# Reordering the loads and the normalising in the first fourteen steps of an attention and key-value kernel

## The chip, the cores and the metric

The kernel runs on one core of one Trainium2 chip. The metric is device time in microseconds (us) of a whole launch; the number that counts is the median of the runs. The engines are named as in the profile: PE (matrix products), DVE (vector), ACT (activations), POOL (general purpose) and SP (which here only issues DMAs).

## The reference

Eight batches of twelve heads of attention with a soft cap, followed by a gated two-layer block on the 8 x 448 rows of 768:

```python
scores = cap * tanh((q @ k.T / sqrt(64)) / cap)           # 8 x 12 x 448 x 448
attn = exp(scores - max); attn = attn / (attn.sum(-1) + 1e-9)
x = (attn @ v) as rows of 12 * 64 = 768
xk = mu_k * x + (1 - mu_k) * x_prev                       # x_prev: the row before
xr = mu_r * x + (1 - mu_r) * x_prev
k = relu(xk @ w_k)                                        # 768 -> 1024
out = sigmoid(xr @ w_r) * (k * k @ w_v)
```

The weights come as 64-bit floats.

## The kernel before

The attention works in 48 pairs of heads, two heads of 448 rows side by side in the partitions. A loop runs over steps i = 0 to 54 (`step`, line 710). What a step does is written out as a string of operation names, and every name emits its instructions at that place, on the queues of the engines that it uses; each engine and each DMA queue works through its own in that order. `STEP_0` serves steps 0 to 5, `STEP_5` step 6, `STEP_6` steps 7 to 13, and `STEP` and `STEP_2` the rest. A name stands for another pair according to the table in `step`: scores (`S`, four groups of keys, three products each of high and low halves), tanh, exp and `red` (sums of exp) take pair i; `V` (the products with v, line 256), `gather`, `recip`, `rec_store` take pair i − 1; `norm` and the mixing take pair i − 2; `qk_high` and `qk_low` split pair i + 2; `load_qk` fetches pair i + 3.

The reciprocal of the row sums takes a way through DRAM: DVE's `red` (line 276) sums over blocks of 32, four DMAs on SP's queue gather them (`gather`, line 283, waiting for the last `red`), DVE adds up, takes reciprocals and transposes (`recip`, line 287), SP stores 3.5 KB to DRAM (`rec_store`) and loads it back spread over the partitions in two DMAs (`rec_load`, line 298; one buffer). `norm` (line 304, DVE) multiplies the products with v by it, `mix_old` (line 307, ACT) and `mix_new` (line 317, DVE) mix neighbouring rows, and POOL splits the result (`x_high`, `x_low`) for the second part.

Beside this a step converts one piece of the weights: load (`weight_load`, SP), absolute value (`weight_abs`, ACT), five roundings on DVE (`fill`, written f in the string), sum and copy on POOL (`weight_sum`, line 469), low half on DVE at the head of the next step (`weight_low`, line 483). The first six pieces have 384 columns, the next ones 768. The first weight piece goes through the roundings in step 0 (`weight_first`).

PE does scores and `V`; from the end of step 6 on it also does `K`, 24 products a step with the first weight matrix, from the mixed rows of six pairs. In steps 7 to 13 its order within a step is scores 0 and 1, `V`, scores 2, K, K, scores 3, K, K. The score buffers are two: scores 0 and 1 of a step need tanh 2 and tanh 3 of the one before. A second stage after the attention multiplies by the other two weight matrices, on PE nearly alone; `out_store` (line 623) writes the result from SP's queue.

Of the kernel before, what the change touches and what calls it, by code (L numbers as in the profile page):

```python
# [10 lines left out]
F32 = mybir.dt.float32  # L11
F32R = mybir.dt.float32r
AF = mybir.ActivationFunctionType
ALU = mybir.AluOpType
# [11 lines left out]
HN = DM // 2  # L26
NU = NT // 256
SLOTS = 7
AHEAD = 2
P = 128  # L30
U32 = mybir.dt.uint32
CAP = 50.0
# [21 lines left out]

STEP = """gather load_v quad_load x_store weight_load weight_low S0 S1 V S2 f f f f f tanh0 exp0 red0
weight_sum tanh1 exp1 red1 norm recip rec_store K qk_high qk_low tanh2 relu mix_old k_store prep mix_new x_high x_low gate_old
K exp2 red2 weight_rest weight_sum relu k_store prep S3 K prep K tanh3 exp3 red3 gate_new relu k_store prep
weight_abs load_qk rec_load quad_load tail_open weight_store"""  # L60
STEP_2 = STEP.replace("K qk_high", "K S3 qk_high").replace("prep S3 K", "prep K")
STEP_0 = """gather load_v x_store weight_load weight_low S0 S1 S2 V f f f f f norm tanh0 exp0 red0 weight_first
weight_sum tanh1 exp1 red1 recip rec_store K qk_high qk_low tanh2 relu exp2 mix_old k_store mix_new x_high x_low gate_old
K red2 weight_rest weight_sum relu k_store S3 K K tanh3 exp3 red3 gate_new relu k_store weight_abs load_qk rec_load weight_store"""
STEP_6 = """gather load_v x_store weight_load weight_low S0 S1 V S2 f f f f f norm tanh0 exp0 red0
weight_sum tanh1 exp1 K relu_early qk_rise tanh2 relu exp2 mix_old k_store mix_new red1 recip rec_store qk_low x_high x_low gate_old
K red2 weight_rest weight_sum relu k_store S3 K K tanh3 exp3 red3 gate_new relu k_store weight_abs load_qk rec_load weight_store"""
STEP_5 = STEP_6.replace("V S2", "S2 V")


def f(ap):
# [3 lines left out]
class Body:  # L75
# [30 lines left out]
    def scale(self, pool):  # L106
        nc = self.nc
        self.scl_t = pool.tile([P, 1], F32, name="scl_t")
        nc.vector.reciprocal(self.scl_t, self.cap_t)
        nc.vector.tensor_scalar(self.scl_t, self.scl_t, D ** -0.5, None, op0=ALU.mult)  # L110

    def consts(self, pool):
        nc = self.nc
        self.mu, self.om = {}, {}
        for n, src in (("k", self.muk), ("r", self.mur)):
            m = pool.tile([P, ND], F32, name="mu_" + n)
            nc.sync.dma_start(m, src)
            o = pool.tile([P, ND], F32, name="om_" + n)
            nc.vector.tensor_scalar(o, m, -1.0, 1.0, op0=ALU.mult, op1=ALU.add)
            self.mu[n], self.om[n] = m, o  # L120
        self.grd = pool.tile([P, 1], F32, name="grd")
        if self.maxima:
            nc.vector.memset(self.grd, 1e-9)
            return
        sq = pool.tile([1, 1], F32, name="sq")
        nc.vector.tensor_mul(sq, self.cap_t[0:1], self.cap_t[0:1])
        nc.vector.tensor_scalar(self.flag, sq, CAP * CAP, None, op0=ALU.is_le)
        nc.vector.tensor_scalar(self.cap_t, self.cap_t, -CAP, CAP, op0=ALU.max, op1=ALU.min)

        nc.scalar.activation(self.grd, self.cap_t, AF.Abs)  # L130
        nc.scalar.activation(self.grd, self.grd, AF.Exp, scale=-1.0)
        nc.vector.tensor_scalar(self.grd, self.grd, 1e-9, None, op0=ALU.mult)


    def init_x(self, pool):
# [23 lines left out]

    def init_attn(self):  # L160
        self.raw, self.QK, self.rawv, self.S, self.P32, self.PV, self.R, self.rs = ({} for _ in range(8))
        self.tails = []

# [128 lines left out]

    def rec_store(self, i):
        self.nc.sync.dma_start(self.rec_d[i].rearrange("h (b k) -> (h b) k", k=32), self.rs.pop(i)[0:NB])

    def rec_load(self, i):
        r = self.up.tile([P, S], F32, name="r", bufs=1)
        for h in range(2):  # L300
            self.nc.sync.dma_start(r[HALF[h]], self.rec_d[i][h:h + 1, :].to_broadcast([64, S]))
        self.R[i] = r
# [320 lines left out]
    def out_store(self, u, key, o, g):  # L623
        self.nc.vector.tensor_mul(o, g, self.vl.pop((u, key)))
        t = ((u - NU) * 2 + key // 2) * P
        self.nc.sync.dma_start(self.out[t:t + P, key % 2 * HN:(key % 2 + 1) * HN], o)

    def v_load(self, u, key):
        t = self.vl[u, key] = self.ldp.tile([P, HN], F32, name="vl", bufs=6)
# [80 lines left out]
    def step(self, i, KS):  # L710

        nk = nq = 0
        if self.maxima and i < NPAIR:
            self.row_maxima(i)
        pair = dict(load_qk=i + 3, qk_high=i + 2, qk_low=i + 2, qk_rise=i + 2, load_v=i, S=i, tanh=i, exp=i, red=i)
        pair.update(dict.fromkeys("V gather recip rec_store rec_load".split(), i - 1))
        pair.update(dict.fromkeys("norm mix_old mix_new x_high x_low gate_old gate_new".split(), i - 2))
        pair["x_store"] = i - 3
        for op in (STEP_0 if i < 6 else STEP_5 if i == 6 else STEP_6 if i < REST[0] else STEP_2 if i % NP == 2 else STEP).split():
            j = pair.get(op)  # L720
            op, g = (op[:-1], (int(op[-1]),)) if op[-1].isdigit() else (op, ())
            if op in pair:
                j = pair[op] if j is None else j
                if i == NPAIR + 1 and op in ("x_high", "x_low"):
                    g = ("s",) if op == "x_high" else ("v",)
                if 0 <= j < NPAIR:
                    getattr(self, dict(S="scores", V="values").get(op, op))(j, *g)
            elif op == "K":
                n = ((i - LAG) * 4 + nk + 1) * KS
                if 0 <= n < B * NF * ND * 3:  # L730
                    self.kpart(n, n + KS)
                nk += 1
            elif op == "tail_open":
                self.tail_open(i)
            elif op == "f":
                if i in (QUADS + 3, QUADS + 5):
                    self.quad_sum(i - QUADS - 3)
                elif i <= NPAIR:
                    self.fill()
            elif op == "quad_load":  # L740
                if QUADS <= i < QUADS + 4:
                    self.quad_load(2 * (i - QUADS) + nq)
                    nq += 1
            elif op == "relu_early":
                if i % NP == 2:
                    self.relu()
            elif op == "weight_load":
                if i + 1 in KEYS or i + 1 in REST:
                    self.weight_load()
            elif op == "weight_first":  # L750
                if i == 0:
                    self.weight_abs()
                    self.weight_rest()
            elif op == "weight_abs":
                if i in KEYS or i in REST:
                    self.weight_abs()
            else:
                getattr(self, op)()

    def run(self):  # L760
        tc, nc = self.tc, self.nc
# [6 lines left out]
        with ExitStack() as outer:  # L768
            def pool(name, bufs, stack=outer, **kw):
                return stack.enter_context(tc.tile_pool(name=name, bufs=bufs, **kw))  # L770
# [9 lines left out]
            cpool = pool("cpool", 1)  # L780
# [20 lines left out]
            first = self.qk_first()  # L801
            self.cap_load(cpool)
            self.load_part(0, slice(S + P, S + KC))
            self.weight_load()
            next(first)
            self.scale(cpool)
            next(first)
            self.consts(cpool)
            self.init_sums(self.xkp[0])
            self.load_qk(1)  # L810
            self.qk_high(1)
            self.qk_low(1)
            self.init_guard()
            self.load_qk(2)
            self.weight_load()
            self.wgen = self.weight_round()
# [124 lines left out]
```

## Time and profile before

| what | us |
|---|---|
| median of three runs (922.75 to 924.2) | 922.76 |
| the profiled execution | 921.6 |
| its span, from the first to the last instruction | 919.7 |
| PE busy in it | 891.4 |
| DVE busy | 739.3 |
| ACT busy | 643.5 |
| POOL busy | 384.8 |

The shares of busy time are averages over two parts of different kind: the attention with the first weight matrix, up to 554 us, with all engines at work, and the second stage. The change is in the first 135 us and at the last store, so the profile is read there by stretches, and PE's 97% of the whole says little about it.

### The profile page before, as it was taken

The page shows a single profiled execution, that of the slowest core. Times are in us where ns is not written, and L with a number is a line of the kernel's source. Part 1 is how long each engine was busy: PE and PEld are TensorE (multiplying, and loading weights), DVE is VectorE, ACT ScalarE, POOL GpSimd, SP SyncE. Part 2 cuts the span into 40 slices and gives each one's busy share as a digit, 9 for nine tenths or more (in the row PEclk, how much of TensorE's full clock was granted, in tenths as well). Part 3 has the DMA queues.
Part 4 walks back from the last instruction along what each step waited for, and adds up shares of the span by engine and source line. Part 5 has one row for each costly group of instructions (what it writes and reads, how often), then busy time and mean ns, then how long its engine had stood idle before and what let it go on. Part 6 is the DMA issues. An engine that isn't in the chain of part 4 may idle for free.

```text
span 919.7 us, 15134 instructions
## 1 busy us (share of the span) xinstructions
PE 891.4 (97%) x4986; PEld 716.0 (78%) x4986; DVE 739.3 (80%) x1253; ACT 643.5 (70%) x949; POOL 384.8 (42%) x332
## 2 busy tenths in 40 slices
PE   6879999999999999999999999999999999999996
PEld 3335677666666776666677799999999999999996
DVE  6999977888888888888878866788778767777775
ACT  7978888888887887888877666565565535555553
POOL 4655554776676676666764300000000014443330
PEclk9989999999999999999999999999999999999998
DMA  5565544666566666666656474745454646666663
GB/s 180 153 188 187 187 143 159 223 214 202 197 194 209 213 192 207 207 193 205 196 187 194 128 237 153 234 158 170 154 168 143 189 134 192 217 219 219 218 214 104
DMA packets 123656, 171.95 MB, mean 187 GB/s; under 512 B 22576, under 2 KB 107696, under 8 KB 123568
## 3 DMA queue, kind: packets, MB, share of 16 engines
q1 hardware_dynamic: 114352, 156.21, 54.2%
q10 hardware_dynamic: 9216, 14.68, 4.3%
q8 instruction: 41, 0.67, 0.3%
q14 instruction: 47, 0.39, 0.1%
HBM read 111.48 MB, written 56.60 MB: 183 GB/s over the span
## 4 chain that ended last, share of the span: by engine, by line
PE 88%; DVE 5%; DMA 3%; ACT 2%; issue 1%; SPq 0%; DVEq 0%; ACTq 0%
PE ps L586 39%; PE kps L394 24%; PE s L236 12%; PE pv L263 10%; DVE r L280 2%; PE pv L271 2%; DMA rec_d<-rs 1%; DMA r<-rec_d 1%; ACT p L244 1%; PE s L394 1%; ACT p L254 0%; DMA mu_k<-muk 0%; DVE wkl L485 0%; DVE sr L289 0%; DMA rv<-v 0%
## 5 line engine op out<-in xcount | busy, mean ns | idle before, releaser
L280 DVE TRANSPOSE_TENSOR_REDUCE r<-p 128x28 f32<-128x896 f32 (+1 forms) x240 | 217.4, 916 | 23.8 <-ACT p L254 19.3
L244 ACT ACTIVATE p<-s,scl_t 128x896 f32<-128x896 f32 x192 | 173.3, 902 | 29.5 <-PE s L236 26.0
L254 ACT ACTIVATE p<-p,cap_t 128x896 f32<-128x896 f32 x192 | 182.1, 949 | 5.6 <-ACT pv L315 0.5
L394 PE MATMUL kps<-xkh,wkh 128*128 128x448 f32 x372 | 140.3, 377 | 0.0
L394 PE MATMUL kps<-xkl,wkh 128*128 128x448 f32 x372 | 136.0, 366 | 0.0
L394 PE MATMUL kps<-xkh,wkl 128*128 128x448 f32 x372 | 136.0, 366 | 0.0
L586 PE MATMUL ps<-wvh,hi 128*128 128x384 f32 x392 | 131.0, 334 | 0.0
L586 PE MATMUL ps<-wvl,hi 128*128 128x384 f32 x392 | 130.9, 334 | 0.0
L570 ACT CAST hi<-s 128x512 fp32r<-128x512 f32 (+1 forms) x112 | 63.6, 568 | 88.7 <-PE ps L586 76.5
L550 POOL TENSOR_TENSOR s<-src 128x384 f32<-128x384 f32 x14 | 14.3, 1019 | 266.3 <-DVE lo L571 266.3
L263 PE MATMUL pv<-p,rv 128*64 128x448 f32 x576 | 124.0, 567 | 1.7 <-DMA rv<-v 1.7
L571 DVE TENSOR_TENSOR lo<-s,hi 128x512 fp32r<-128x512 f32 (+1 forms) x112 | 70.8, 632 | 58.8 <-ACT hi L570 43.5
L99 POOL TENSOR_TENSOR qkl<-rqk,qkh 128x960 fp32r<-128x960 f32 x47 | 107.1, 2279 | 15.4 <-ACT qkh L93 12.1
L236 PE MATMUL s<-qkh 64*128 64x448 f32 (+1 forms) x336 | 84.2, 443 | 18.3 <-ACT p L244 13.4
L586 PE MATMUL ps<-wrh,hi 128*128 128x384 f32 x294 | 98.6, 335 | 0.3 <-DVE o L609 0.3
L586 PE MATMUL ps<-wrl,hi 128*128 128x384 f32 x294 | 98.5, 335 | 0.0
L471 POOL TENSOR_TENSOR wsq<-wa,wsq 128x384 f32<-128x384 f32 (+1 forms) x39 | 43.7, 1121 | 127.2 <-DVE wsq L464 99.3
L236 PEld LDWEIGHTS s<-qkh 64*128 64x128 f32 (+1 forms) x336 | 36.7, 188 | 75.5 <-ACT p L244 32.8
L570 ACT CAST hi<-src 128x512 fp32r<-128x512 f32 (+1 forms) x84 | 47.6, 567 | 62.3 <-PE ps L586 59.1
L263 PEld LDWEIGHTS pv<-p,rv 128*64 128x64 f32 x576 | 38.8, 141 | 64.4 <-issue 58.0
L394 PEld LDWEIGHTS kps<-xkh,wkh 128*128 128x128 f32 x372 | 69.7, 187 | 18.9 <-issue 11.9
L586 PE MATMUL ps<-wvh,lo 128*128 128x384 f32 x392 | 83.7, 334 | 0.0
(103 smaller groups left out, 1789.5 us busy)
## 6 DMA issues: line engine op xcount, KB each, us to landing
rqk<-qk SPq DMA_DIRECT2D x47, 480.0 KB
k_d<-ko ACTq DMA_DIRECT2D x64, 224.0 KB
src<-k_d SPq DMA_DIRECT2D x56, 256.0 KB
rv<-v SPq DMA_DIRECT2D x48, 256.0 KB
r<-rec_d SPq DMA_DIRECT2D x96, 112.0 KB
v_d<-o SPq DMA_DIRECT2D x56, 192.0 KB
src<-x_d SPq DMA_DIRECT2D x42, 256.0 KB
vl<-v_d SPq DMA_DIRECT2D x56, 192.0 KB
```

The lines of the kernel that those rows point to most:

```text
L99: {"p": self.nc.gpsimd, "v": self.nc.vector}[e].tensor_sub(*a)
L236: nc.tensor.matmul(s[:, h, 0:S], qk[a][p, k], qk[b][p, 0:S], start=(n == 0), stop=(n == 2))
L244: self.nc.scalar.activation(p32, self.S.pop((i, g))[:, :n, 0:S], AF.Tanh, scale=self.scl_t)
L254: self.nc.scalar.activation(p32, p32, AF.Exp, scale=1.0 if self.maxima else self.cap_t)
L263: nc.tensor.matmul(pv[p, 0:S], v[:, g, h, :], ph[:, h, :], start=(g == 0), stop=False)
L271: nc.tensor.matmul(self.PV[j][p, 0:S], v[t, 3, h, :], ph[t, 0, :], start=False, stop=True)
L280: self.nc.vector.tensor_reduce(out=out, in_=p32[p, h].rearrange("p h (b k) -> p (h b) k", k=32), axis=mybir.AxisListType.X, op=ALU.add, ap ...
L394: nc.tensor.matmul(self.kps[fc][:, 0:S], w, m[:, dc, :], start=first, stop=last)
L471: {"p": self.nc.gpsimd, "v": self.nc.vector}[e].tensor_add(sq, f(a), sq)
L570: self.nc.scalar.copy(hi, x)
L571: self.nc.vector.tensor_sub(lo, x, f(hi))
L586: self.nc.tensor.matmul(o, a[:, c, :], w[:, c, :], start=first and k == 0, stop=last and k == len(todo) - 1, skip_group_check=True)
```

## The change

In steps 0 to 13 the load of the reciprocals (`rec_load`) and that of q and k (`load_qk`) leave the end of a step. They now stand at the head of the next: `rec_load` directly behind `gather`, `load_qk` behind `load_v`. `rec_load` takes the pair that was stored last; in the steps from 14 on it stays at the end (in step 14 it is done at both places). `norm` moves behind the second sum (`red1`). In `STEP_6` `red1`, `recip` and `rec_store` move ahead of tanh 2. The sum of the first weight piece on POOL is held back until after the split of pair 2. Ahead of the steps, the guard against small sums (a constant of the cap, on DVE and ACT) comes before the mixing constants, and q and k of pair 1 are loaded ahead of the first weight piece, the mixing constants behind it. The very last store of the result is issued by ACT in place of SP.

```diff
 STEP = """gather rec_load load_v quad_load x_store weight_load weight_low S0 S1 V S2 f f f f f tanh0 exp0 red0
...
-STEP_0 = """gather load_v x_store weight_load weight_low S0 S1 S2 V f f f f f norm tanh0 exp0 red0 weight_first
-weight_sum tanh1 exp1 red1 recip rec_store K qk_high qk_low tanh2 relu exp2 mix_old k_store mix_new x_high x_low gate_old
-K red2 weight_rest weight_sum relu k_store S3 K K tanh3 exp3 red3 gate_new relu k_store weight_abs load_qk rec_load weight_store"""
-STEP_6 = """gather load_v x_store weight_load weight_low S0 S1 V S2 f f f f f norm tanh0 exp0 red0
-weight_sum tanh1 exp1 K relu_early qk_rise tanh2 relu exp2 mix_old k_store mix_new red1 recip rec_store qk_low x_high x_low gate_old
-K red2 weight_rest weight_sum relu k_store S3 K K tanh3 exp3 red3 gate_new relu k_store weight_abs load_qk rec_load weight_store"""
+STEP_0 = """gather rec_load load_v load_qk x_store weight_load weight_low S0 S1 S2 V f f f f f tanh0 exp0 red0 weight_first
+weight_sum tanh1 exp1 red1 norm recip rec_store K qk_high qk_low tanh2 relu exp2 mix_old k_store mix_new x_high x_low gate_old
+K red2 weight_rest weight_sum relu k_store S3 K K tanh3 exp3 red3 gate_new relu k_store weight_abs weight_store"""
+STEP_6 = """gather rec_load load_v load_qk x_store weight_load weight_low S0 S1 V S2 f f f f f tanh0 exp0 red0
+weight_sum tanh1 exp1 K relu_early qk_rise red1 norm recip rec_store tanh2 relu exp2 mix_old k_store mix_new qk_low x_high x_low gate_old
+K red2 weight_rest weight_sum relu k_store S3 K K tanh3 exp3 red3 gate_new relu k_store weight_abs weight_store"""
...
     def rec_store(self, i):
         self.nc.sync.dma_start(self.rec_d[i].rearrange("h (b k) -> (h b) k", k=32), self.rs.pop(i)[0:NB])
+        self.stored.append(i)
...
-    def rec_load(self, i):
+    def rec_load(self):
+        if not self.stored:
+            return
+        i = self.stored.pop()
...
-        self.nc.sync.dma_start(self.out[t:t + P, key % 2 * HN:(key % 2 + 1) * HN], o)
+        queue = self.nc.scalar if (u, key) == (2 * NU - 1, 0) else self.nc.sync
+        queue.dma_start(self.out[t:t + P, key % 2 * HN:(key % 2 + 1) * HN], o)
...
                 if i == 0:
                     self.weight_abs()
                     self.weight_rest()
+                    self.w_sum, held = [], self.w_sum
+            elif op == "weight_rest" and i == 0:
+                self.w_sum = held
...
             self.load_part(0, slice(S + P, S + KC))
+            self.load_qk(1)
             self.weight_load()
             next(first)
             self.scale(cpool)
             next(first)
-            self.consts(cpool)
+            self.guard()
             self.init_sums(self.xkp[0])
-            self.load_qk(1)
             self.qk_high(1)
             self.qk_low(1)
             self.init_guard()
+            self.consts(cpool)
             self.load_qk(2)
```

What `guard` and `scale` emit stood in `consts` before (lines 121 to 132).

## Rows read from the trace of the kernel before

**Rows 1.** Windows by stage: us, busy (instructions) of each engine, clock, DMA share, GB/s.
```profile
0.00:17.00 17.00, 9.58 (x35) 5.40 (x37) 9.96 (x24) 12.03 (x17) 7.82 (x18) 1.00 0.64 201
17.00:65.90 48.90, 39.70 (x195) 16.64 (x195) 45.95 (x80) 42.06 (x52) 32.24 (x29) 0.95 0.55 162
65.90:123.60 57.70, 54.25 (x297) 34.28 (x293) 54.03 (x82) 48.94 (x60) 32.49 (x25) 0.99 0.56 177
123.60:912.40 788.80, 787.91 (x4467) 659.71 (x4463) 628.80 (x1071) 540.48 (x823) 312.26 (x262) 1.00 0.60 190
```
**Rows 2.** Windows by step of DVE: steps 2, 3, 5, 7 and 10.
```profile
27.21:36.72 9.51, 7.90 (x47) 3.61 (x49) 9.02 (x18) 9.35 (x13) 6.41 (x6) 1.00 0.53 158
36.72:45.98 9.26, 7.79 (x47) 3.34 (x45) 9.03 (x17) 9.10 (x12) 6.13 (x6) 1.00 0.64 192
...
55.55:65.89 10.34, 7.95 (x37) 3.28 (x35) 9.11 (x16) 8.12 (x11) 6.55 (x7) 0.83 0.57 168
...
77.28:88.44 11.16, 10.83 (x63) 7.09 (x59) 10.92 (x17) 9.27 (x12) 6.30 (x5) 1.00 0.63 185
...
112.57:123.56 10.99, 10.99 (x65) 7.68 (x63) 10.72 (x18) 9.96 (x13) 6.19 (x5) 1.00 0.44 136
```
**Rows 3.** Waits in 17 to 124 us: who for whom, total, times, longest.
```profile
DVE x L305 <- DMA r<-rec_d: 2.8, 4, 1.0
...
ACT qkh L93 <- DMA rqk<-qk: 5.2, 4, 1.8
```
**Rows 4.** Timeline of step 3: start, us, engine, line, operation, count.
```profile
36.79 2.44 SPq L285 DMA_DIRECT2D sq<-r  x4
...
39.43 0.63 DVE L305 TENSOR_TENSOR x<-pv,r 128x448 f32<-128x448 f32 x1
...
39.98 2.10 DVE L280 TRANSPOSE_TENSOR_REDUCE r<-p 128x28 f32<-128x896 f32 x2
...
41.99 0.56 DVE L289 TENSOR_REDUCE sr<-sq 32x28 f32<-32x448 f32 x1
```
**Rows 5.** Chain of waits in 50 to 125 us: start, us, what.
```profile
56.22 3.01 DMA r<-rec_d
...
67.25 0.48 SPq L301
...
67.79 2.89 DMA r<-rec_d
...
119.29 1.46 PE s L236 x12
```
**Rows 6.** Timeline of steps 0 and 1.
```profile
7.48 0.99 ACT L244 ACTIVATE p<-s,scl_t 128x896 f32<-128x896 f32 x1
...
13.75 3.29 DVE L280 TRANSPOSE_TENSOR_REDUCE r<-p 128x28 f32<-128x896 f32 x4
...
15.54 1.00 POOL L89 TENSOR_SCALAR qkh<-rqk 128x960 fp32r<-128x960 f32 x1
16.43 2.50 SPq L285 DMA_DIRECT2D sq<-r  x4
...
16.62 2.23 POOL L99 TENSOR_TENSOR qkl<-rqk,qkh 128x960 fp32r<-128x960 f32 x1
...
17.07 2.20 DVE L485 TENSOR_TENSOR wkl<-wsq,wkh 128x384 fp32r<-128x384 f32 x1
```
**Rows 7.** Timeline of step 10, DVE and ACT.
```profile
117.04 0.62 DVE L305 TENSOR_TENSOR x<-pv,r 128x448 f32<-128x448 f32 x1
...
119.20 0.64 ACT L244 ACTIVATE p<-s,scl_t 128x448 f32<-128x448 f32 x1 [0.40 <-ACT ko L401]
```
**Rows 8.** Timeline of SP at the end.
```profile
912.46 0.33 SPq L626 DMA_DIRECT2D out<-o  x1
912.96 2.08 SPq L626 DMA_DIRECT2D out<-o  x1
```
**Rows 9.** Waits of SP in 905 to 920 us.
```profile
SPq L894 <- SPq L894: 2.7, 1, 2.7
```

More of the change, by code (lines that the diff above doesn't have):

```diff
@@ L50 @@
 LATE = [*range(12), NPAIR - 2, NPAIR - 1]
-STEP = """gather load_v quad_load x_store weight_load weight_low S0 S1 V S2 f f f f f tanh0 exp0 red0
+STEP = """gather rec_load load_v quad_load x_store weight_load weight_low S0 S1 V S2 f f f f f tanh0 exp0 red0
 weight_sum tanh1 exp1 red1 norm recip rec_store K qk_high qk_low tanh2 relu mix_old k_store prep mix_new x_high x_low gate_old
@@ L110, in scale, with guard @@
         nc.vector.tensor_scalar(self.scl_t, self.scl_t, D ** -0.5, None, op0=ALU.mult)
+        self.grd = pool.tile([P, 1], F32, name="grd")
+        if self.maxima:
+            return
+        sq = pool.tile([1, 1], F32, name="sq")
+        nc.vector.tensor_mul(sq, self.cap_t[0:1], self.cap_t[0:1])
+        nc.vector.tensor_scalar(self.flag, sq, CAP * CAP, None, op0=ALU.is_le)
+        nc.vector.tensor_scalar(self.cap_t, self.cap_t, -CAP, CAP, op0=ALU.max, op1=ALU.min)
+    def guard(self):
+        nc = self.nc
+        if self.maxima:
+            nc.vector.memset(self.grd, 1e-9)
+            return
+        nc.scalar.activation(self.grd, self.cap_t, AF.Abs)
+        nc.scalar.activation(self.grd, self.grd, AF.Exp, scale=-1.0)
+        nc.vector.tensor_scalar(self.grd, self.grd, 1e-9, None, op0=ALU.mult)
     def consts(self, pool):
@@ L120, in consts @@
             self.mu[n], self.om[n] = m, o
[L121 to L132, printed above, removed]
     def init_x(self, pool):
@@ L161, in init_attn @@
         self.raw, self.QK, self.rawv, self.S, self.P32, self.PV, self.R, self.rs = ({} for _ in range(8))
-        self.tails = []
+        self.tails, self.stored = [], []
     def load_qk(self, i):
@@ L296, in rec_store @@
         self.nc.sync.dma_start(self.rec_d[i].rearrange("h (b k) -> (h b) k", k=32), self.rs.pop(i)[0:NB])
-    def rec_load(self, i):
+        self.stored.append(i)
+    def rec_load(self):
+        if not self.stored:
+            return
+        i = self.stored.pop()
         r = self.up.tile([P, S], F32, name="r", bufs=1)
@@ L715, in step @@
         pair = dict(load_qk=i + 3, qk_high=i + 2, qk_low=i + 2, qk_rise=i + 2, load_v=i, S=i, tanh=i, exp=i, red=i)
-        pair.update(dict.fromkeys("V gather recip rec_store rec_load".split(), i - 1))
+        pair.update(dict.fromkeys("V gather recip rec_store".split(), i - 1))
         pair.update(dict.fromkeys("norm mix_old mix_new x_high x_low gate_old gate_new".split(), i - 2))
```

## The prediction

> **What bounds the kernel now.** First I read the busy times by stage, to see which engine has no idle time where. From 123.6 to 912.4 us PE is busy for 787.9 of 788.8 us, and the change touches none of that but the very last store; so it is worth what it does to the moment at which PE becomes dense, plus what it does behind PE's last product [rows 1]. Before that moment PE has gaps: 9.2 us in 17 to 65.9 and 3.5 us in 65.9 to 123.6, while DVE is busy for 94% of both stretches [rows 1]. The second view is the same cut at the steps. I mark a step by T, the moment when DVE has done its last sum and begins the weights' low half (line 485). Steps 3 and 7 show DVE packed: 9.26 us with half-size weight pieces, 11.16 with whole ones [rows 2]. Steps 2 to 5 together take 38.7 us (27.21 to 65.89), steps 6 to 10 take 57.7 (65.89 to 123.56) [rows 2]. The third view, the waits, names what is lacking in steps 1 to 10: DVE waits 2.8 us for the broadcast reciprocals, and ACT 5.2 us for q and k [rows 3]. ACT's wait lies beside DVE's work, so taking it away alone moves nothing while DVE paces.
>
> The change adds and removes no instruction; every cost below is one of order.
>
> **Start, steps 0 and 1.** The first tanh starts at 7.48 us, since the clamped cap sits behind the mixing constants on DVE [rows 6]. With the guard ahead of them, ACT goes on when its last cast of q and k is through, some 1.4 us earlier (estimate; the two guard activations and that tanh then follow the cast). This alone doesn't end step 1 sooner: the held weight sum comes behind POOL's cast and subtraction of pair 2, whose load DMA brings at about 12.3 us (estimate: some 2.46 MB issued up to there at the 201 GB/s of that time [rows 1]; bounds 9.3 us, with the bytes ahead alone, and 15.5, when POOL's cast starts today [rows 6]). POOL then needs 1.0 and 2.23 us for these [rows 6] and by their columns 1.3 for sum and copy, with gaps until about 17.4. DVE's low half waits for that, idle since 15.6 (today its sums end at 17.04 [rows 6]). But it no longer runs beside POOL's subtraction: today it starts at 17.07 and takes 2.20 us, until POOL's instruction of 2.23 us has ended [rows 6]; I take 0.5, since in step 3 it and five roundings take 2.71 together [rows 2, 4]. So the roundings of step 1 begin at 17.9 in place of 19.2, and the mark T of step 1 comes at 25.85 in place of 27.21: **1.35 us gained** (bounds: 0.4 lost, 2.6 gained). The Trainium skill's page "SBUF — State Buffer", section "SBUF: two separate sides", says that DVE with two operands in SBUF and GpSimd shut each other out for a whole instruction; these 2.20 us agree, and by its rule the held sum would save the whole difference of 1.7 us on that instruction.
>
> **Steps 2 to 5: the reciprocals come later.** Today their load stands ahead of the gather in SP's queue; the change puts it behind, and v, q, k, the store and the weights behind both. A gather is four issues in 2.5 us from 36.79 on [rows 4]; the second half of the reciprocals is issued 0.54 us after the first and lands 2.9 to 3.0 us later [rows 5]. From T: 0.07 until the gather starts, 2.5, 0.54, 2.85, and 0.1 to wake DVE, so the normalising can begin at T + 6.05. Where the gathered pair is even, its first half needs the first of the last two sums only: gather 0 starts at 16.43, before the sums end at 17.04 [rows 6]; then it is T + 5.36. DVE itself has 2.71 us of weights (36.72 to 39.43) and two sums of 2.01 us (39.98 to 41.99) ahead of the normalising in the new order, and arrives at T + 4.72 [rows 4]. It therefore waits 1.3 us in steps 2 and 4 and 0.6 in steps 3 and 5, with reciprocal, mixing and two sums queued behind. These follow the normalising's 0.55 and take 3.99 (41.99 to 45.98) [rows 2, 4]. Steps: 10.6, 9.9, 10.6, 9.9, in all 41.0 in place of 38.7: **2.3 us lost**. Bounds: no wait at all (9.26 each, 1.6 gained) and 0.75 more in each, if the transfers queue behind others (5.3 lost). I take the landing of the rows, because nothing but the small gathers is ahead of these loads then.
>
> **Steps 6 to 10: the waits go.** With whole pieces DVE arrives at T + 6.55, after the reciprocals. ACT's mixing follows the normalising at once and DVE's own mixing comes 1.1 us behind it, so neither waits. Step 6 has one half-size subtraction left (10.8, estimate), steps 7 to 9 take 11.16 and step 10 takes 11.0: 55.3 in place of 57.7, **2.4 us gained** (bounds 1.0 and 2.4). q and k, issued a step ahead of their use, end ACT's 5.2 us of waits [rows 3]. The buffer that they need was freed by POOL one step before, so SP isn't held by it, except at step 0, where the third weight load stands behind it until POOL has split pair 1; its use is two steps away. T of step 9 comes at 111.1 in place of 112.57.
>
> **What PE gets.** The normalising behind the second sum makes ACT's last part later within a step. In step 10 it starts at 117.04 today (T + 4.47), ACT waits for it, and tanh 3 ends at 119.84, 2.8 us on; PE's two score products of step 11 run from 119.29 to 120.75 without a break, the second from 120.02 [rows 5, 7]. After: normalising at T + 6.55 = 117.65, tanh 3 done 2.8 us later, the second product from 120.5. PE is dense from there: in step 10 it was busy for all of 10.99 us [rows 2], longer than the new chain from sum to sum (10.6 and 9.9). **0.5 us lost** at the entry to the dense stage, though T came 1.45 us sooner.
>
> **The end.** SP issues the last store at 912.96 and takes 2.08 us for it, where the one ahead took 0.33; then SP's branch needs 2.7 us more [rows 8, 9]. On ACT's queue, empty then, I take 0.33 for it, and SP can branch 1.75 to 2.2 us sooner, until the stores' landing takes over. I take **1.4 us gained** (bounds 0 and 2.2).
>
> **Sum.** The profiled execution took 921.6 us, its span of 919.7 and 1.9 around it: 921.6 + 0.5 − 1.4 = 920.7. The median of the runs stands 1.2 above it, so I predict 921.8. About 0.2% (1.85 us) is what a measurement of this kernel can tell from no change.
>
> **Rivals.**
> *The reciprocals are there in time* (faster). If they land 1.3 us sooner than today's rows say, none of the steps waits, T of step 9 comes at 107.5 and PE could be at its scores over 3 us earlier; it can't gain more than the 3.5 us that it idles from 65.9 to 123.6 [rows 1]. I take 3.4: 921.8 − 0.5 − 3.4 = 917.9; half of that is enough for 919.9. For it: the queue is emptier than today when they are issued, and step 1 may come earlier too. Against it: 2.89 and 3.01 us are landings with nothing large ahead [rows 5].
> *The burst at the head of the step* (slower). v, q and k, a store and a weight piece, 1.73 MB from step 4 on, are now issued together at T + 3.7. If they move at under some 175 GB/s, they still run when the next reciprocals are issued (10.6 + 3.0 − 3.7 = 9.9 us later), and these queue behind them. In 17 to 65.9 the mean was 162 GB/s, in 65.9 to 123.6 it was 177, though idle time is in both means [rows 1]. Price: 0.75 us in each of steps 2 to 5 and 0.4 in each of 6 to 10, 5 us: 926.8; in steps 4 to 10 alone 925.3.
> *The landing and not the issue ends the kernel* (no gain there). SP then waits for the last store as long as today: 921.8 + 1.4 = 923.2. The rows speak against it, since SP's own branch comes behind the 2.08 us [rows 8, 9]. The Trainium skill, page "DMA: Bandwidth & Descriptors", section "Issuing engines are not separate DMA queues", says that a second issuing engine saves only the sequencer's time and brings no byte sooner; by it this rival holds if the bytes are last, and the forecast if SP's sequencer is.
> *Steps 0 to 10 show nothing*: PE's own work takes up gain and loss, and the end alone remains: 921.8 − 0.5 = 921.3.
>
> **How the numbers follow.** Forecast 0.33, with the two rivals that stay within 0.2% (0.06 and 0.04) 0.43 in all. The reciprocals in time, wholly or in part: 0.34, faster. The burst: 0.23, slower. The range takes in part of both, from 918.4 (most of the faster rival) to 925.4 (the burst from step 4 on), and leaves out about 0.1 on each side. The likeliest case's own range is 920.6 to 924.2.
>
> **What would show it.** Right: no ACT wait for q and k; the gather starting with DVE's mark; DVE waiting about 1.3 and 0.6 us in turn for the reciprocals in steps 2 to 5 and not in 6 to 10; the low half of step 1 at 17.4 and 0.5 us long; step 10 ending near 122; PE dense from 120.5; ACT issuing the last store in 0.33. Wrong: steps 2 to 5 at 9.3 us (then faster), reciprocals landing over 3.2 us after their issue (then slower), or the end of the kernel no nearer to the last product.

## The result

The changed kernel is slower. Its median is 927.9 us (five runs, 927.2 to 930.5) beside 922.7 for the kernel before on the same chip: a ratio of 1.0061, interval 1.0043 to 1.0079. The prediction was 921.8, and the median lies 2.5 us above the top of its range. The profiled execution took 930.5 us (span 928.6), 2.6 above the median, so its absolute losses are a little larger than the typical ones.

I read it in the order of the prediction. First the windows by stage, cut at T of steps 0, 1, 5 and 10 and at 180 us (columns as in [rows 1]):

```profile
19.74:27.87 8.13, 6.96 (x43) 2.96 (x39) 7.89 (x14) 6.42 (x8) 4.74 (x4) 1.00 0.47 149
27.87:71.50 43.63, 30.02 (x136) 12.69 (x134) 36.38 (x66) 30.51 (x39) 25.60 (x24) 0.79 0.53 165
71.50:128.38 56.88, 55.61 (x295) 34.42 (x297) 54.53 (x81) 49.12 (x60) 32.91 (x25) 0.95 0.55 176
128.38:180.00 51.62, 49.57 (x270) 32.99 (x267) 33.55 (x51) 40.68 (x51) 20.93 (x17) 0.97 0.52 164
180.00:922.50 742.50, 742.15 (x4208) 627.70 (x4207) 594.94 (x1019) 500.63 (x774) 290.71 (x245) 1.00 0.60 190
```

Steps 2 to 5 take 43.6 us (before 38.7), and DVE, the engine that paced them, is busy for 83% where it was 94% [rows 1]. Steps 6 to 10 take 56.9 (before 57.7). PE is not dense from step 11 on: 2.05 us are missing between 128 and 180. From 180 us on it is dense.

The waits from 17 to 124 us, to be read beside [rows 3] (engine and line, whom it waited for, total, times, longest):

```profile
ACT pv L324 <- DVE x L314: 16.4, 8, 5.7
PE s L241 <- ACT p L249: 15.0, 10, 6.1
DVE x L314 <- DMA r<-rec_d: 5.9, 4, 2.4
```

ACT's waits for q and k are gone. DVE now waits 5.9 us for the reciprocals, ACT waits behind that at its mixing, and PE behind ACT. How one step turns over is in the chain of waits, here step 4 from its gather on (start, us, what; T of step 3 is at 49.77):

```profile
49.20 0.64 DVE r L285
...
52.41 0.54 SPq L310
...
52.99 3.25 DMA r<-rec_d
...
56.36 0.64 DVE x L314
57.02 0.64 ACT pv L324
57.66 0.56 ACT p L249
...
60.31 1.44 PE s L241 x6
```

From the normalising on DVE works without a pause, through reciprocal, mixing and three sums, until the next T at 60.91. So the chain comes back to its start: last sum, four issues of the gather, load of the reciprocals, normalising, DVE's work behind it, next last sum. It is a ring, 10.2 to 11.7 us long in steps 2 to 5, and DVE's 9.3 us of work in a step are no longer the limit. ACT's mixing and fourth tanh, for which PE's scores wait, are a branch of it. The ring still turns in steps 11 to 14, where I had called PE dense:

```profile
142.23 3.18 DMA r<-rec_d
...
164.56 3.93 DMA r<-rec_d
168.58 0.64 DVE x L314
169.24 0.65 ACT pv L324
...
171.20 0.53 ACT p L249
171.77 0.87 PE s L241 x6
172.64 4.10 PE pv L268 x12
```

At 171.77 PE has been idle for 2.05 us, and its clock falls: these twelve products take 4.10 us. The window of them (columns as above) has a mean granted clock of 0.58, so of the two levels, 2.4 and 1.2 GHz, it was mostly at the lower:

```profile
172.64:176.74 4.10, 4.10 (x16) 1.13 (x14) 3.52 (x8) 3.63 (x6) 1.51 (x2) 0.58 0.55 180
```

In e2 below, where PE idles for 1.00 us at that place, the same twelve take 2.40 us:

```profile
171.75 2.40 PE pv L270 x12
```

### The profile page after: what moved, and what is told of

Same layout as the page of the kernel before. It is cut to its first block, busy times and chain, and to the rows that moved or that the text cites. A ratio compares the mean times of both kernels' runs of the same rounds, so it can differ in the third digit from the quotient of the medians.

```text
span 928.6 us, 15118 instructions
## 1 busy us (share of the span) xinstructions
PE 897.5 (97%) x4986; PEld 717.7 (77%) x4986; DVE 741.9 (80%) x1253; ACT 643.4 (69%) x949; POOL 384.2 (41%) x332
## 4 chain that ended last, share of the span: by engine, by line
PE 81%; DVE 8%; DMA 5%; SPq 2%; issue 1%; POOL 1%; ACT 1%; DVEq 0%; ACTq 0%; POOLq 0%
PE ps L595 38%; PE kps L403 21%; PE s L241 10%; PE pv L268 9%; DMA r<-rec_d 3%; DVE r L285 3%; PE pv L276 2%; SPq L290 1%; PE s L403 1%; SPq L310 1%; DVE wkl L494 1%; DMA k_d<-ko 1%; DMA rec_d<-rs 1%; DVE sr L294 1%; DMA mu_k<-muk 1%
## 5 line engine op out<-in xcount | busy, mean ns | idle before, releaser
L268 PE MATMUL pv<-p,rv 128*64 128x448 f32 x576 | 128.2, 583 | 0.0
L241 PEld LDWEIGHTS s<-qkh 64*128 64x128 f32 (+1 forms) x336 | 37.1, 190 | 82.3 <-ACT p L249 37.7
L480 POOL TENSOR_TENSOR wsq<-wa,wsq 128x384 f32<-128x384 f32 (+1 forms) x39 | 43.6, 1119 | 129.2 <-DVE wsq L473 107.6
L268 PEld LDWEIGHTS pv<-p,rv 128*64 128x64 f32 x576 | 39.3, 144 | 65.9 <-issue 60.9
```

The source lines that it names most:

```text
L241: nc.tensor.matmul(s[:, h, 0:S], qk[a][p, k], qk[b][p, 0:S], start=(n == 0), stop=(n == 2))
L268: nc.tensor.matmul(pv[p, 0:S], v[:, g, h, :], ph[:, h, :], start=(g == 0), stop=False)
L480: {"p": self.nc.gpsimd, "v": self.nc.vector}[e].tensor_add(sq, f(a), sq)
```

## The experiments

All times are medians; "before" ran beside every group and had 922.1 to 922.9, and differences between kernels of two groups are no surer than that. The table has, from each kernel's profiled execution, the time of steps 2 to 5 and 6 to 10 (from T to T on DVE) and PE's idle time between 124 and 180 us.

| kernel | median us | ratio to before (interval) | steps 2–5 | 6–10 | PE idle |
|---|---|---|---|---|---|
| before | 922.7 | | 38.7 | 57.7 | 0.0 |
| changed | 927.9 | 1.0061 (1.0043 to 1.0079) | 43.6 | 56.9 | 2.9 |
| e1_load_ahead | 929.1 | 1.0063 (1.0043 to 1.0083) | 42.8 | 60.7 | 0.9 |
| e2_old_start | 927.0 | 1.0044 (1.0029 to 1.0059) | 43.5 | 56.9 | 2.2 |
| e3_store_act | 921.5 | 0.9980 (0.9969 to 0.9991) | 38.9 | 57.9 | 0.0 |
| e4_ahead_old_start | 928.0 | 1.0051 (1.0031 to 1.0071) | 42.4 | 60.1 | 0.0 |
| f1_qk_end | 932.0 | 1.0102 (1.0081 to 1.0123) | 42.8 | 57.0 | 4.2 |
| f2_qk_head | 927.6 | 1.0057 (1.0041 to 1.0073) | 43.2 | 59.0 | 0.0 |
| f3_norm_late | 921.1 | 0.9984 (0.9971 to 0.9996) | 39.3 | 56.1 | 0.0 |
| f4_store_on_act | 923.9 | 1.0010 (0.9997 to 1.0022) | 41.1 | 58.1 | 0.2 |
| g1_guard_early | 922.1 | 0.9999 (0.9990 to 1.0009) | 39.4 | 56.2 | 0.0 |
| g2_guard_held | 921.7 | 0.9987 (0.9976 to 0.9999) | 39.4 | 56.2 | 0.0 |
| g3_weights_behind | 920.5 | 0.9977 (0.9968 to 0.9986) | 37.7 | 56.3 | 0.0 |
| g4_gather_split | 920.5 | 0.9981 (0.9971 to 0.9991) | 38.6 | 56.1 | 0.0 |
| h1_square | 930.6 | 1.0093 (1.0066 to 1.0120) | 42.9 | 57.7 | 3.0 |
| h3_square_split | 921.2 | 0.9987 (0.9974 to 1.0001) | 38.9 | 56.3 | 0.0 |
| h2_best_start | 919.9 | 0.9966 (0.9953 to 0.9978) | 38.3 | 56.2 | 0.0 |

### First group: undo the suspect

**e1_load_ahead**: in the changed kernel's step strings

```diff
-gather rec_load load_v ...
+rec_load gather load_v ...
```


> The changed kernel with one swap: at the head of each step the reciprocals' load stands ahead of the gather in SP's queue again, all else as changed. Theory (the place of that load behind the gather is the main cost): the second half lands near T + 3 in place of T + 5.5 to 7, DVE doesn't wait for it in steps 2 to 5, these four take 38 to 39.5 us in place of 43.6, TensorE's low clock in steps 2 to 5 goes for the most part, its 2 us gap of step 14 goes, and the time is 920 to 922.5. Rival one (the start with its new order of first loads is the main cost): T of step 1 stays at 27.9, and the time stays at 926 or above. Rival two (the burst of q, k, v and weights at the head of the step makes the reciprocals late): their landing stays at 3.0 to 3.25 us after issue or gets longer, DVE still waits, and the time is 925 or above.

929.1 us: the theory fell (steps 2 to 5 take 42.8 us, where it had 38 to 39.5). The reciprocals are loaded ahead of the gather again, and nothing is won; T of step 1 is 27.59, and DVE still waits 3.4 us for them.

**e2_old_start**: the start as before (constants' load and clamped cap in their old places, no held weight sum).

```diff
-            self.load_qk(1)
             self.weight_load()
...
+            self.consts(cpool)
+            self.clampcap(cpool)
             self.guard()
             self.init_sums(self.xkp[0])
+            self.load_qk(1)
...
-            self.consts(cpool)
```


> The changed kernel with the start of the kernel before: the mixing constants' load ahead of pair 1's q and k, the clamped cap and the guard behind them, and the first weight sum not held back. All steps' orders as changed. Theory (the load behind the gather is the main cost, and the start lost 0.7 us instead of gaining 1.4): T of step 1 back near 27.2, steps 2 to 5 still at 43 us, and the time 926 to 927.5. Rival one (the start is the main cost): the time falls to 923 or below.

927.0 us, in the theory's range, with steps 2 to 5 at 43.5; T of step 1 is 27.66. The start costs 0.9 us beside the changed kernel, less than the spread of either's runs.

**e3_store_act**: the kernel before with the last store on ACT's queue, the last lines of the change's diff alone.

> The kernel before with only the very last output store moved from SP's to ACT's queue. By the traces the span's end comes 4.9 us behind DVE's last product in place of 6.8: the time 920.9, between 920.6 and 921.4. Rival (the gain of the changed kernel's end belongs to its profiled run alone): 922.5 to 923.

921.5 us, 1.35 below before: the end's term, at nearly the forecast's 1.4.

**e4_ahead_old_start**: the edits of e1 and e2 together.

> The changed kernel with both undone: the reciprocals' load ahead of the gather and the old start. What is left of the change is q and k at the head of the step, the normalising behind the second sum in steps 0 to 13, and the last store on ACT's queue. Theory (load behind the gather is the main cost and the start a small one): 919.5 to 921.5, by 0.5 to 0.7 below the kernel with the load alone put back. Rival two (the burst at the head, or the normalising behind the second sum, costs by itself): 923.5 or above in spite of the 1.8 us that the store gives.

928.0 us, and beside e1 again 1.1 for the start. Some 6.5 us over e3 stay in what was left, as rival two had it: q and k at the head, or the late normalising. Its chain of waits shows the place:

```profile
54.37 0.21 DVE rs L300
...
54.60 5.38 DMA rec_d<-rs
...
60.00 0.48 SPq L312
...
62.88 1.04 SPq L292
...
63.98 1.76 DMA sq<-r
...
65.81 0.62 DVE sr L296
```

The reciprocals' store of 3.5 KB takes 5.38 us. SP, which comes to the load next, waits for it, and with SP the gather behind it (line 292 here), for whose landing DVE's next reciprocal waits. In the same step of the kernel before the store needed 2.92 us. What SP had issued ahead is in its timeline (start, us, line, operation, count):

```profile
52.19 0.54 SPq L183 DMA_DIRECT2D rv<-v  x1
52.77 0.42 SPq L179 DMA_DIRECT2D rqk<-qk  x1
53.24 0.43 SPq L362 DMA_DIRECT2D raw_d<-x  x1
53.77 0.38 SPq L436 DMA_DIRECT2D w<-wk  x1
54.60 0.35 SPq L303 DMA_DIRECT2D rec_d<-rs  x1
60.00 1.12 SPq L312 DMA_DIRECT2D r<-rec_d  x2
```

So a new theory: a second ring, reciprocal, store, load, next normalising and reciprocal, or, as in the lines above, with SP's issues of load and gather and the gather's landing in place of the load's. It paces when the burst at the head of the step is ahead of the store. The kernel before is near it already; in its chain of waits stand, each ahead of a landing of the load [rows 5],

```profile
52.75 2.92 DMA rec_d<-rs
...
63.09 4.15 DMA rec_d<-rs
```

10.34 us apart, which is the length of its step 5 [rows 2]. The prediction read the load's landings there and not the store's. In all, SP waits 16.4 us for the store in 17 to 124 us in the kernel before, and 37.6 in e4.

### Second group: each part alone

**f1_qk_end**: the changed kernel with

```diff
-gather rec_load load_v load_qk x_store ...   ... weight_abs weight_store
+gather rec_load load_v x_store ...           ... weight_abs load_qk weight_store
```


> The changed kernel with q and k loaded at the end of the step again, behind the reciprocals' store in SP's queue; the reciprocals' load stays behind the gather. New theory: the changed kernel holds two costs that hide one another. One is the load behind the gather, which by itself makes the normalising late (T + 5.5 to 7). The other is q and k at the head, which puts 0.49 MB more ahead of the small store of the reciprocals, and SP then waits for that store's landing: 4.8 to 6.1 us where it was 1.6 to 3.2. By it this kernel keeps the first cost and loses the second, and is at 924.5 to 927.5, with the store's landing at 1.6 to 3 us. Rival one (q and k at the head is the whole cost): 923 or below. Rival two (the normalising behind the second sum is the cost): 926 or above and steps 2 to 5 as in the changed kernel, without waits of SP for the store.

932.0 us, 4.5 above the theory's range: the load behind the gather is dear by itself, more so than with q and k at the head. That rival two has the time right is undone by f3 below.

**f2_qk_head**: e3 with the opposite.

```diff
-gather load_v x_store ...           ... weight_abs load_qk rec_load weight_store
+gather load_v load_qk x_store ...   ... weight_abs rec_load weight_store
```


> The kernel before with two edits: the last store on ACT's queue (worth 1.35 us by itself, 921.5) and q and k at the head of the step, behind the gather and v; the normalising ahead of the first sum and the reciprocals' load as before. New theory (the burst holds the reciprocals' store, SP waits for it, and the gather behind it comes late): the store takes 4.5 to 6 us to land from step 3 on in place of 1.6 to 3.2, steps 4 to 10 get longer, and the time is 925 to 929. Rival (q and k at the head cost nothing, the normalising behind the second sum does): 920.5 to 922.

927.6 us: 6.1 over e3 for moving one load, in the theory's range. The store lands 3.0 to 6.0 us behind its issue in steps 3 to 8 (the theory had 4.5 to 6; e3 has 1.3 to 5.2), and SP waits 25.8 us for it in 17 to 124 us (e3: 16.7). In the chain of waits it is the longest piece in steps 4, 5, 7 and 8:

```profile
54.50 4.10 DMA rec_d<-rs
...
67.08 3.69 DMA rec_d<-rs
...
90.00 4.07 DMA rec_d<-rs
...
101.82 6.03 DMA rec_d<-rs
```

**f3_norm_late**: e3 with

```diff
-f f f f f norm tanh0 ... red1 recip rec_store
+f f f f f tanh0 ...      red1 norm recip rec_store
```


> The kernel before with two edits: the last store on ACT's queue (921.5 by itself) and the normalising with reciprocal and their store behind the second sum in steps 0 to 13. Loads as before. New theory (this edit costs at most what PE's entry into the dense stage loses, and takes DVE's waits for the reciprocals away): 920.5 to 922.5. Rival (it is the main cost, as ACT's mixing comes later in each step and TensorE waits for ACT): 925 or above.

921.1 us. The late normalising costs nothing (e4 beside f2 says the same, 928.0 and 927.6), and steps 6 to 10 take 56.1, 1.6 less than before of the 2.4 that were forecast for them.

**f4_store_on_act**: e4 with, in steps 0 to 13,

```diff
-red1 norm recip rec_store ... tanh3 exp3
+red1 norm recip ...           tanh3 rec_store exp3
...
-        self.nc.sync.dma_start(self.rec_d[i]...
+        queue = self.nc.scalar if i < REST[0] - 1 else self.nc.sync
+        queue.dma_start(self.rec_d[i]...
```


> As the kernel with the reciprocals' load ahead of the gather and the old start (928.0), with one more edit: in steps 0 to 13 the reciprocals' store is issued on ACT's queue, behind that step's fourth tanh, in place of SP's. New theory, first form (the store waits for its turn behind the loads of its own queue): on another queue it lands 1.6 to 2.2 us after its issue whatever SP has in flight, SP isn't held, steps 3 to 5 take 9.3 to 10 us each, and the time is 919.5 to 922. Second form (the store waits because the DMA engines are busy with the loads, whatever the queue): it still takes 4 us or more, and the time stays at 926 to 929.

Neither form as written. By the trace the store still lands 2.7 to 6.4 us behind its issue in steps 2 to 8 (median 4.9; e4 5.2), so it is not the order within SP's queue that holds it. Yet the time fell by 4.2 to 923.9, though SP waits even longer for the store (52.1 us in 17 to 124, e4 37.6); so SP's waiting alone does not set the price. DVE waits 0.7 in place of 3.8 us for the reciprocals, and the seven landings of the store come to 33.4 in place of 37.7 us. Whether that is the 4.2 is not shown. The Trainium skill, page "DMA: Bandwidth & Descriptors", section "Issuing engines are not separate DMA queues", says that DMAs of all issuing engines run on the same 16 engines; a landing of 4.9 beside 5.2 us agrees.

### Third group: one cause taken away at a time

**g3_weights_behind**: e4 with the bytes ahead of the store cut, q and k staying at the head.

```diff
-rec_load gather load_v load_qk x_store weight_load ... recip rec_store
+rec_load gather load_v load_qk ...                     recip rec_store x_store weight_load
```


> As the kernel with the reciprocals' load ahead of the gather and the old start (928.0), with x's store and the weight load of steps 0 to 13 moved behind the reciprocals' store; q and k stay at the head. New theory (what delays the reciprocals' store is the sum of bytes that the DMA engines still have, whoever issued them; its round trip through DRAM then paces the steps): 0.4 to 0.8 MB less are ahead, the store lands 1.3 to 3 us after its issue, steps 3 to 5 take 9.2 to 10 us, and the time is 920.5 to 924. Rival (q and k at the head cost by something else, as their own buffer's wait holding SP): 926.5 or above.

920.5 us, 7.5 below e4. SP's timeline in the same step as above:

```profile
48.45 0.53 SPq L183 DMA_DIRECT2D rv<-v  x1
49.08 0.38 SPq L179 DMA_DIRECT2D rqk<-qk  x1
52.22 0.34 SPq L303 DMA_DIRECT2D rec_d<-rs  x1
52.61 0.35 SPq L362 DMA_DIRECT2D raw_d<-x  x1
53.08 0.38 SPq L436 DMA_DIRECT2D w<-wk  x1
53.56 1.61 SPq L312 DMA_DIRECT2D r<-rec_d  x2
```

The store has landed when SP comes to the load, 1.34 us after its issue, and in 17 to 124 us SP waits 3.3 us for it where it was 37.6. It is the bytes ahead of it and not q and k as such; the load itself takes longer now (4.3 us for this step's second half in the trace), and that does no harm.

**g4_gather_split**: e2 with half of the gather on ACT's queue in steps 0 to 13.

```diff
-gather rec_load ... tanh0 exp0 red0
+gather rec_load ... tanh0 exp0 gather_act red0
...
-        for q in range(4):
+        for q in range(4 if i >= REST[0] - 1 else 2):
...
+    def gather_act(self, i):
+        for q in range(2, 4):
+            self.nc.scalar.dma_start(self.sq[i % 2][:, q], self.r1[i % 2][32 * q:32 * q + 32])
```


> As the changed kernel with the old start (927.0: reciprocals' load behind the gather, q and k at the head), with the last two of the gather's four issues on ACT's queue in steps 0 to 13, behind that step's first exp. Theory (with the load behind the gather the loop sums, gather's issues, load, normalising, mixing, sums paces; the four issues are 2.4 us of it): the load is issued 1.1 to 1.2 us sooner after T, steps 2 to 5 take 9.3 to 9.9 us in place of 10.6 to 11.3, and the time is 921.5 to 924.5. Rival (the store's landing paces here too, and the load only waits for that): 926 or above.

920.5 us, 6.5 below e2, with the load still behind what is left of the gather. The first ring is shown by this: two issues of 0.6 us each out of it, and steps 2 to 5 go from 43.5 to 38.6. SP's timeline, T of this step being 45.91:

```profile
46.01 1.18 SPq L292 DMA_DIRECT2D sq<-r  x2
47.28 1.30 SPq L316 DMA_DIRECT2D r<-rec_d  x2
```

**g1_guard_early** and **g2_guard_held**: f3 with the guard ahead of the constants' arithmetic, the constants' load staying ahead of pair 1's q and k; g2 also holds the first weight sum as the change does.

```diff
             next(first)
+            self.guard()
             self.consts(cpool)
             self.init_sums(self.xkp[0])
             self.load_qk(1)
```


> The kernel with the late normalising and the last store on ACT's queue (921.1; loads in the order of before), and of the changed start only the clamped cap and the guard ahead of the mixing constants on DVE; the constants' load stays ahead of pair 1's q and k in SP's queue. Theory (the changed start loses since the mixing constants land late and hold DVE, not by the guard's place): the first tanh at 6.3 us as in the changed kernel, the constants' second operand not waited for beyond 8 us, T of step 0 at 16 to 17, of step 1 at 25.7 to 26.7, and the time 919.8 to 921.0. Rival (the guard's place itself loses, or DVE and POOL exclude one another at the start): 921.8 or above.

> The same with the first weight sum held back behind POOL's split of pair 2, as in the changed kernel. By the prediction's working the low half of step 1 then runs without POOL beside it (0.5 in place of 2.2 us), T of step 1 comes up to 1.2 us earlier than without holding, and the time is 919 to 920.5. Rival (holding only moves DVE's wait from POOL's instruction to the held sum): within 0.5 us of the kernel without it.

922.1 and 921.7: no gain over f3's 921.1, and g2 within 0.5 us of g1, as its rival had it. The first sum of g1 starts at 8.16, where f3's starts at 10.08, but T of step 0 moves only from 16.97 to 16.66: the rival, in its second form. DVE's timeline of g1 shows why (start, us, line, operation):

```profile
9.20 0.32 DVE L461 TENSOR_SCALAR wsq<-wsq 128x384 f32<-128x384 f32 x1
9.55 2.27 DVE L463 TENSOR_SCALAR wa<-wsq 128x384 uint32<-128x384 uint32 x1
```

The second rounding, 0.36 elsewhere, takes 2.27, beside POOL's subtraction of pair 1 (9.22, 2.38 us).

### Fourth group: what was left

**h1_square** is e2 with f1's edit, **h3_square_split** that with g4's edit.

> The changed kernel with the old start and with q and k loaded at the end of the step, behind the reciprocals' store; the reciprocals' load stays behind the gather. It is the fourth cell beside 921.1 (load ahead, q and k at the end), 928.0 (ahead, head) and 927.0 (behind, head). Theory (q and k, issued just ahead of the gather and the reciprocals' load, lie in the DMA engines when that load comes, so it takes 3.6 to 4.1 us in place of 3.0, and the loop that it closes is longer by that in each step): 929.5 to 931.5, with PE's idle time behind 124 us at 3 us or more. Rival (that kernel's excess was its start): 926 to 927.5.

> The same kernel with the gather's last two issues on ACT's queue behind the first exp. Theory (the excess is in the loop sums, gather, load, normalising, sums; the split takes 1.2 us out of each turn): steps 2 to 5 at 9.3 to 10 us, PE's idle time behind 124 us gone or under 0.5 us, and the time 920.5 to 924. Rival (the excess is elsewhere, as in the reach of q and k or of the values): 926 or above.

930.6 and 921.2 us. With the old start in all, the square is: load ahead of the gather, q and k at the end 921.1; ahead, head 928.0; behind, end 930.6; behind, head 927.0. So the load behind the gather costs 9.5 us by itself, q and k at the head 6.9, and both together 5.9, not the 16.4 of their sum. The split takes 9.4 out of the dearest cell, so its excess lies in the first ring. That q and k make the load longer there is not shown: its second half took 3.3 us on the mean of steps 11 to 14 in h1 (3.44, 3.75, 2.77, 3.26) and 3.1 in e2 (2.78, 3.36, 3.42, 2.79). The profiled execution of h1 was the fastest of its six, 928.0 us, as long as that of e2 (928.1), so these two traces can't show what the medians differ by.

**h2_best_start**: g3's loads with g2's start.

> The fastest order of the loads (load ahead of the gather, q and k at the head, x's store and weights behind the reciprocals' store; 920.5) with the clamped cap and guard ahead of the mixing constants and the first weight sum held back, the constants' load staying where it was. Theory (the start is worth T of step 1 some 0.6 us sooner, and PE's dense stage follows at most that): 919.6 to 920.6. Rival (PE or the first rounds of DVE take it up): no difference, 920.3 to 921.

919.9 us, ratio 0.9966 (0.9953 to 0.9978): faster than both kernels, by 2.8 us than before on the same chip. T of step 1 comes at 25.98 where g3 has 26.70, and 0.6 of that shows in the median, within the spread of the runs.

## Why the prediction was wrong

| term | forecast us | measured in the profiled execution |
|---|---|---|
| T of step 1 | 25.85 | 27.87 |
| steps 2 to 5 | 41.0 | 43.6 |
| steps 6 to 10 | 55.3 | 56.9 |
| PE's idle time behind that | 0 | 2.05, and a fall of the clock (1.7) |
| the end | 1.4 gained | 1.84 gained (the span ends 4.94 behind DVE's last product, before 6.78) |

**The start: the sign was wrong.** The first tanh did come at 6.33 as worked out. But I costed only the guard's move and the held sum. That the constants' load itself was moved, behind pair 1's q and k and a weight piece, stood at nothing in the sum, without a reason:

```profile
8.20 2.23 POOL L100 TENSOR_TENSOR qkl<-rqk,qkh 128x960 fp32r<-128x960 f32 x1
...
8.31 2.13 DVE L136 TENSOR_SCALAR om_k<-mu_k 128x6 f32<-128x6 f32 x1 [1.58 <-DMA mu_k<-muk]
...
10.43 1.10 DVE L285 TRANSPOSE_TENSOR_REDUCE r<-p 128x28 f32<-128x896 f32 x1
```

DVE waits 1.58 us for them, and its six columns then take 2.13 us, ending when POOL's subtraction does. The Trainium skill, page "SBUF — State Buffer", section "SBUF: two separate sides", says that of an instruction of DVE and one of GpSimd that both use the shared port pair, the one that starts first has it for its whole length; these rows, POOL's first by 0.11 us and both at their end at 10.4, agree. A second one follows (12.63, 2.29 us, a rounding beside POOL's subtraction of pair 2). The held low half took 0.56, as forecast, at 19.74 and not 17.4. Undone alone, the start gives 0.9, 1.1 and 1.4 us (the changed kernel beside e2, e1 beside e4, f1 beside h1), each within the spread of the runs and all three the same way. T of one trace can't decide it: in the eleven traces with the old order of the start T of step 1 lies between 26.69 and 27.89. The guard and the holding alone cost nothing that can be told (g1, g2), and with the constants' load in its old place T of step 1 comes at 26.07 (g2) and 25.98 (h2), close to the forecast 25.85; so what costs is the order of the loads. That follows from the difference; the load was not moved by itself.

**Steps 2 to 5: the mechanism was right, the size not.** The gather starts 0.1 us behind T in steps 2 and 4 and 0.7 ahead of it in 3 and 5, as worked out, and the loss of 4.95 lies inside the bounds. DVE waits 2.4, 0.8 and 1.8 us for the reciprocals in steps 2 to 4, where 1.3 and 0.6 stood, and in step 5 1.2 us, which its row puts down to PE's products. The sum was closed as a ring, from T over the normalising to the next T, and its second part holds: from the normalising to the next T it is 4.55 or 4.56 us in all four steps, where 4.54 stood. The step that failed is the first part, gather and load: the normalising begins at T + 7.18, 5.61, 6.59 and 6.03, where T + 6.05 and T + 5.36 stood, 2.6 us more in all. Some 1.0 of this is the landing of the load's second half, 3.00, 3.04, 3.25 and 3.09 us for 2.85, a figure under both of the rows that it was taken from (2.89 and 3.01) [rows 5]. Another 0.9 is one issue of the load in step 2, with 0.54 in the sum:

```profile
30.50 1.40 SPq L310
...
31.93 3.00 DMA r<-rec_d
```

Why it took so long no run shows. The last 0.4 is mostly a gather of 2.9 us in step 5.

**Steps 6 to 10: a gain of 0.8 in place of 2.4 us.** f3, with the late normalising and the loads as before, takes 56.1 us, so half of the miss is DVE's own step: it reaches the normalising at T + 6.8 in steps 8 to 10, where 6.55 stood. The other half is step 6, 11.55 us in place of f3's 10.59, where the store of the reciprocals took 5.93 us to land, SP's load came behind it, and DVE waited 0.8 us.

**PE dense from step 11: wrong for the reason of steps 2 to 5.** I compared the new chain (10.6 and 9.9) with PE's 11 us of work. From one normalising to the next it took 10.4, 11.6, 10.4 and 12.7 us in steps 11 to 14, with nothing to spare; in step 14, where the first issue of the load took 1.42 us and the landing 3.93, PE stands for 2.05 us and runs at the lower clock behind it.

**The end was right**, in the changed kernel and alone (e3: 1.35).

**The rivals.** The burst came nearest in time, 926.8, and by a place of which I had not thought. I let it delay the load of the reciprocals; what it delays is their store, a step earlier. In the changed kernel that store has the gather's time to land in and holds SP for 1.1 us in all; in e4 and f2 it paces. "The reciprocals are there in time" was refuted by the landings; "nothing shows" and "the landing ends the kernel" by the square and by e3. That moving the load behind the gather might be the answer to q and k at the head, and so can't be judged alone, did not occur to me.

Still open are why the load behind the gather costs 3.6 us more without q and k at the head, and what f4's 4.2 us are made of. The 10.7 us by which PE ends later in the profiled execution are nearly all placed: 4.8 are there at T of step 10, 2.05 are idle time behind it, 1.7 the clock (4.10 less 2.40), and 2.1 more work behind that T, 4477 products where the kernel before has 4467. That last part comes with the late normalising: in f3 PE is busy for 789.6 us behind T of step 10, before for 787.9. The prediction had it, with T 1.4 us sooner and PE 0.5 later.

## What to carry to other kernels

A value that goes through DRAM and comes back to the same engine one step later closes a ring: add up every issue, store, load and instruction of it, and compare the sum with the pace of the busiest engine; in steps 2 to 5 here, what the ring had above that was added to the step. Where the sum is within a few tenths of that pace, ask how much one landing or one issue varies in the rows (2.8 to 3.9 and 0.5 to 1.4 us here) before calling the wait hidden. Before moving a large load, look at which small transfer is issued behind it and who waits for that one; 0.49 MB moved by some microseconds cost 6 us here, and moving other bytes behind the store gave it all back. Two edits that each lose can together lose less than their sum (9.5 and 6.9, and 5.9 together), so test both halves and not only the whole.

## What the runs showed of the hardware

- A store of 3.5 KB needed 1.27 us when little was in flight (g3) and up to 7.5 behind a burst (e4), on another engine's queue up to 6.4 (f4).
- A DVE instruction of six columns took 2.13 us, and roundings of 0.36 took 2.27 and 2.29, each ending at most 0.2 us behind a POOL subtraction that ran beside it; which DVE instruction is hit depends on the order, but in every order of the start tried one was.
- The granted clock by itself says little about such a stretch. In h2, the fastest kernel, its mean in steps 1 to 5 was 0.84, lower than the 0.92 of f3:

```profile
17.00:64.28 47.28, 38.40 (x179) 15.97 (x175) 44.72 (x79) 38.49 (x48) 31.09 (x30) 0.84 0.54 165
```

DVE, busy for 95% of it, paced there.
